# Softmax denominators in four strips of 32 columns, in an attention and feed-forward kernel

## The chip, the cores and the metric

The kernel runs on one core of one Trainium2 chip. The metric is the device time of one launch, in microseconds. A core has five engines that run side by side and wait for one another by semaphores: TensorE (matrix products, PE in the profile), VectorE (DVE), ScalarE (ACT), Pool (GpSimd, POOL) and SyncE (SP, which here issues the transfers).

## The reference

Attention with routing, and a bilinear feed-forward layer on its result. A query sees only the keys that have the same nearest centroid.

```python
batch, n_heads, seq, head_dim, n_clusters = 4, 8, 768, 64, 16     # fp32
# q_n, k_n, c_n: q, k and centroids, each row normalized
q_assign = np.argmax(np.einsum('bhsd,hcd->bhsc', q_n, c_n), axis=-1)
k_assign = np.argmax(np.einsum('bhsd,hcd->bhsc', k_n, c_n), axis=-1)
mask = q_assign[:, :, :, None] == k_assign[:, :, None, :]
scores = np.where(mask, scale * q @ k.T, -1e9)
attn = np.exp(scores - max)
attn = attn / (np.sum(attn, axis=-1, keepdims=True) + 1e-09)
x = (attn @ v)                     # (B,H,S,D) -> (B*S, H*D) = 3072 x 512
out = ((x @ w_a) * (x @ w_b)) @ w_out     # d_ff = 1536
```

What the change touches is the division by `np.sum(attn)`.

## The kernel before: what the change touches

The kernel works through 16 pairs of heads (4 batches, HP = 4 pairs each), each in two halves of HB = 384 queries. Keys lie on the partitions, in NJ = 6 tiles of 128; the two heads `a` of a pair lie side by side. A "group" `g` of the main loop handles two of the twelve key tiles of a pair, so a pair has six groups, and `l` is the group's place in its pair.

For each key tile the scores go through the exponential on ScalarE (`probs`), are summed over the key tiles into `acc` (VectorE, and Pool for later pairs) and are weighed with v on TensorE (line 581). The sum over the 128 keys of a tile is a matrix product with ones (line 604). It leaves the denominator of each query in all of the head's 64 partitions:

```python
def denominators(p, hf):
    ps = ps_m.tile([P, 512], FP32, name="m")
    acc = accs.pop((p, hf))
    terms = [acc]
    if p < HP:                       # first batch: the last key tile isn't in acc
        terms.append(probs[p * UPP + hf * NJ + NJ - 1])
    for n, t in enumerate(terms):
        for a in range(2):
            nc.tensor.matmul(out=ps[a * D:(a + 1) * D, 0:HB], lhsT=ones,      # line 604
                             rhs=t[:, a, :], start=(n == 0),
                             stop=(n == len(terms) - 1))
    den = acc[:, 0, :]
    n = 4 * p + 2 * hf
    nc.scalar.activation(out=den, in_=ps[:, 0:HB], func=AF.Copy,              # line 609
                         accum_out=stat[:, n:n + 1])
    den_of[p, hf] = acc
```

The inverse is then made on few elements. VectorE transposes blocks of 32 x 32, so that 32 equal rows become 32 equal columns, takes the reciprocal of one column of each block, and transposes back from a broadcast. Pool multiplies:

```python
def normalize(p, hf):
    ...
    den, once = acc[:, 0, :], acc[:, 1, :]
    x = xTs[b][:, hp, hf * HB:(hf + 1) * HB]
    inv = small.tile([P, HB // 32], FP32, name="inv")

    def across():
        nc.vector.transpose(out=once, in_=den)                                # line 624
    def invert():
        nc.vector.reciprocal(                                                 # line 627
            out=inv, in_=once.rearrange("p (j t) -> p j t", t=32)[:, :, 0])
    def back():
        nc.vector.transpose(out=den,                                          # line 631
            in_=inv[:, :, None].broadcast_to((P, HB // 32, 32)))
    def apply():
        nc.gpsimd.tensor_tensor(out=x, in0=x, in1=den, op=ALU.mult)           # line 636
        unchecked.append((4 * p + 2 * hf + 1, inv))
    return [across, invert, back, apply]
```

The similarities of queries and keys to the centroids (line 358) already stand in four strips of 32 columns:

```python
for kq in range(4):
    nc.tensor.matmul(out=ps[32 * kq:32 * kq + 32, 0:HB], lhsT=cTb[:, hp, :],  # line 358
                     rhs=qkTs[p][:, kq * HB:(kq + 1) * HB], start=True, stop=True)
```

The main loop (cut) issues small steps from the list `todo`, one after each piece of the feed-forward layer, and the rest at the group's end:

```python
for g in range(NG + 3):
    ...                              # scores, sums (line 570), weighing (line 581)
    if g < NG:
        ready[l]()                   # preparing the next pair; line 358 is here
    late = int(g > EARLY)
    if g % 3 == late and 0 < g - late:
        denominators(*divmod(g // 3 - 1, 2))
    ...
    ph = {first: (p, 0), second: (p - 1, 1)}.get(l)
    halved = ph in den_of
    if halved:
        todo.extend(normalize(*ph))
    if ffn:
        ...
        while len(ffn) > least and credit > 0:
            cost, piece = ffn.popleft()
            credit -= cost
            piece()
            if todo:
                todo.popleft()()
            round_next()
    ...
    while todo:
        todo.popleft()()
    if halved:
        ffn_ready(*ph)               # at a batch's end: its feed-forward pieces
```

At the end of a batch its feed-forward layer begins with combinations of x on VectorE (line 725), which need the normalized x. Its products are lines 664 and 764 (up) and 883 (down). For PSUM there are three buffers `m` that denominators, similarities, transposes and the feed-forward layer share. `acc` has two buffers and `inv` two.

Of the kernel before, what the change touches and what calls it, by code (L numbers as in the profile page):

```python
# [8 lines left out]
FP32 = mybir.dt.float32  # L9
# [4 lines left out]
AF = mybir.ActivationFunctionType  # L14
ALU = mybir.AluOpType
# [15 lines left out]
P = 128  # L31
# [105 lines left out]
def short_path(nc, tc, ctx, c, cn, centroids_in, casts, n_far, q, k, v,  # L137
# [3 lines left out]
    B, H, S, D = q.shape  # L141
# [3 lines left out]
    HP = H // 2  # L145
    NPAIR = B * HP
    NCH = DM // P
    NF = DF // P
    HB = S // 2

    def pool(name, bufs, space=None):
        kw = {} if space is None else {"space": space}
        return ctx.enter_context(tc.tile_pool(name=name, bufs=bufs, **kw))
# [9 lines left out]
    small = pool("small", 2)  # L163
# [11 lines left out]
    ident, identb, ones, rank = c["ident"], c["identb"], c["ones"], c["rank"]  # L175
# [10 lines left out]
    def by_blocks(p):  # L186
        return p >= HP
# [164 lines left out]
    def prep_sim(p):  # L352
# [4 lines left out]
        for kq in range(4):  # L357
            nc.tensor.matmul(out=ps[32 * kq:32 * kq + 32, 0:HB],  # L358
                             lhsT=cTb[:, hp, :],
                             rhs=qkTs[p][:, kq * HB:(kq + 1) * HB],  # L360
                             start=True, stop=True)
        if by_blocks(p):
            sims[p] = ps
            return
        t = simp.tile([P, HB], FP32, name="sim")
        nc.scalar.copy(out=t, in_=ps[:, 0:HB])
        sims[p] = t

    def prep_across(p):
        ps = ps_m.tile([P, 512], FP32, name="m")  # L370
        for t in range(3):
            nc.tensor.transpose(out=ps[:, t * P:(t + 1) * P],
                                in_=sims[p][:, t * P:(t + 1) * P],
                                identity=ident)
        return ps
# [52 lines left out]
    def prep_onehot_first(kq):  # L428
# [3 lines left out]
        for n in (3, 4, 5, 0, 1, 2):  # L432
# [3 lines left out]
                                identity=identb)  # L436
        c0 = kq * HB
        nc.scalar.activation(out=ohTs[0][:, S + c0:S + c0 + HB],
                             in_=ps[:, HB:S], func=AF.Identity, scale=FAR,
# [58 lines left out]
    def prep_steps(p):  # L498
        if p >= NPAIR:
            return [lambda: None] * 6  # L500

        def both(*fs):
            return lambda: [f() for f in fs]

        if by_blocks(p):
            steps = prep_by_blocks(p)
            ready = [lambda s=s: todo.extend(s) for s in steps]
            ready[1] = both(lambda: prep_sim(p), lambda: load_v(p), ready[1])
            return ready

        return [
            both(lambda: prep_transpose(p, 0), lambda: prep_transpose(p, 1)),
            both(lambda: prep_sim(p), lambda: load_v(p)),
            lambda: todo.extend(prep_assign(prep_across(p))),
            lambda: None,
            lambda: prep_onehot(p, 1),
            lambda: None,
        ]
# [2 lines left out]
    probs, accs, O_of, den_of, xTs = {}, {}, {}, {}, {}  # L521
    unchecked = []
    todo = deque()
    UPP = 2 * NJ
    NU = NPAIR * UPP

    def where(u):
        p, l = divmod(u, UPP)
        hf, j = divmod(l, NJ)
        return p, hf, j  # L530

    def score(us):
        tiles = [ps_s.tile([P, 2, 512], FP32, name="s") for _ in us]

        def add(Ts, start):
            for u, s in zip(us, tiles):
                p, hf, j = where(u)
                for a in range(2):
                    r = slice(a * D, (a + 1) * D)
                    nc.tensor.matmul(  # L540
                        out=s[:, a, 0:HB],
                        lhsT=Ts[p][r, S + j * P:S + (j + 1) * P],
                        rhs=Ts[p][r, hf * HB:(hf + 1) * HB],
                        start=start, stop=not start)

        def exp():
            for u, s in zip(us, tiles):
                pt = ptp.tile([P, 2, HB], FP32, name="pt")
                nc.scalar.activation(out=pt, in_=s[:, :, 0:HB], func=AF.Exp,  # L549
                                     scale=SCALE)  # L550
                probs[u] = pt

        if us[0] == 0:
            add(qkTs, True)
            return lambda: [add(ohTs, False), exp()]
        add(ohTs, True)
        add(qkTs, False)
        exp()
# [35 lines left out]
    def denominators(p, hf):  # L594


        ps = ps_m.tile([P, 512], FP32, name="m")
        acc = accs.pop((p, hf))
        terms = [acc]
        if p < HP:  # L600
            terms.append(probs[p * UPP + hf * NJ + NJ - 1])
        for n, t in enumerate(terms):
            for a in range(2):
                nc.tensor.matmul(out=ps[a * D:(a + 1) * D, 0:HB], lhsT=ones,  # L604
                                 rhs=t[:, a, :], start=(n == 0),
                                 stop=(n == len(terms) - 1))
        den = acc[:, 0, :]
        n = 4 * p + 2 * hf
        nc.scalar.activation(out=den, in_=ps[:, 0:HB], func=AF.Copy,
                             accum_out=stat[:, n:n + 1])  # L610
        den_of[p, hf] = acc

    def normalize(p, hf):

        b, hp = divmod(p, HP)
        acc = den_of.pop((p, hf))
        den, once = acc[:, 0, :], acc[:, 1, :]
        x = xTs[b][:, hp, hf * HB:(hf + 1) * HB]
        inv = small.tile([P, HB // 32], FP32, name="inv")

        def across():
            nc.vector.transpose(out=once, in_=den)

        def invert():
            nc.vector.reciprocal(
                out=inv, in_=once.rearrange("p (j t) -> p j t", t=32)[:, :, 0])

        def back():  # L630
            nc.vector.transpose(  # L631
                out=den,
                in_=inv[:, :, None].broadcast_to((P, HB // 32, 32)))

        def apply():
            nc.gpsimd.tensor_tensor(out=x, in0=x, in1=den, op=ALU.mult)  # L636
            unchecked.append((4 * p + 2 * hf + 1, inv))

        return [across, invert, back, apply]

    def check_inverses():
        while unchecked:
            n, inv = unchecked.pop()
            nc.scalar.activation(out=inv, in_=inv, func=AF.Copy,
                                 accum_out=stat[:, n:n + 1])


    ffn = deque()
# [334 lines left out]

    GPP = UPP // 2
    NG = NPAIR * GPP
# [33 lines left out]
    across = prep_across(0)  # L1019
# [10 lines left out]
    for g in range(NG + 3):  # L1030
        p, l = divmod(g, GPP)
        if l == 0:
            ready = prep_steps(p + 1)
        now = (2 * g, 2 * g + 1)
        before = (2 * g - 2, 2 * g - 1)
        if 0 < g < NG:
            score(now)
        check_inverses()
        if 0 < g <= NG:
            for u in before:  # L1040
                add_up(u)
        flush_w()
        if 0 < g <= NG:
            weigh(before)
        if g < NG:
            ready[l]()
        late = int(g > EARLY)
        if g % 3 == late and 0 < g - late:
            denominators(*divmod(g // 3 - 1, 2))
        parts = due.get(g, [])  # L1050

        def round_next():
            if parts:
                i = parts.pop(0)
                round_w(i)
                load_w(i + 2)

        round_next()
        if g <= EARLY:
            first, second = 4, 1  # L1060
        else:
            first, second = 5, 3 if g < NG else 2
        ph = {first: (p, 0), second: (p - 1, 1)}.get(l)
        halved = ph in den_of
        if halved:
            todo.extend(normalize(*ph))
        if ffn:
            credit += PER_GROUP[(g > 2 * BG + 3) + (g > 3 * BG + 3)]
            least = FREE_ROOM if halved and ph[1] and (ph[0] + 1) % HP == 0 else 0
# [7 lines that stand above are left out]
        else:  # L1077
            credit = 0
# [4 lines that stand above are left out]
            ffn_ready(*ph)  # L1083
        if l == 0 and p + 1 < NPAIR:
            if not by_blocks(p + 1):
                prep_transpose(p + 1, 2)
            load(p + 2)
        if l == 4 and p + 1 < NPAIR and not by_blocks(p + 1):
            prep_onehot(p + 1, 0)

    def some_ffn(n):
        for _ in range(n):
# [15 lines left out]
    ps = ps_m.tile([P, 512], FP32, name="m")  # L1108
    nc.tensor.matmul(out=ps[0:1, 0:1], lhsT=far_off, rhs=ones[:, 0:1],
                     start=True, stop=True)  # L1110
# [227 lines left out]
```

## Time and profile before

| | |
|---|---|
| time, median of 3 runs | 1072.6 us (1072.07 to 1073.93) |
| span of the profiled run | 1072.3 us |
| instructions | 13072 |
| mean granted TensorE clock | 0.995 of full speed |
| the denominators' matmuls (line 604) | 160 records, from 30.2 to 875.5 us |
| ScalarE's eviction of them (line 609) | 32, 489 ns each |
| VectorE's transpose (line 624) | 32, 568 ns each |
| reciprocal (line 627) | 32, 221 ns each |
| transpose back (line 631) | 32, 574 ns each |
| Pool's product (line 636) | 32, 1033 ns each |

How to read the profile: in a group such as `m<-acc,ones 128*64 128x384` the output stands left of the arrow and the inputs right of it; 128\*64 are the rows and columns of the array that the matrix product uses, 128x384 the partitions and columns that stream through it. A product of fp32 leaves two records in the trace. Records of matmuls overlap, so the time of a group is read from the start of the next one, not from its length. "Idle before" with an arrow names what the engine waited for. The chain of work is followed back from the last instruction: at each step to what released it.

### The profile page before, as it was taken

What the parts mean: (1) busy time and instruction counts of PE and PEld (TensorE: products, weight loads), DVE (VectorE), ACT (ScalarE), POOL (GpSimd) and SP (SyncE); (2) the same over time, 40 slices, a digit from 0 to 9 for tenths busy, and PEclk for the clock granted to TensorE, in tenths of its full rate; (3) what the DMA queues carried; (4) which work ended last, traced back from release to release, by engine and by line L of the source; (5) the groups of instructions that cost most, each with busy time, mean ns of one, the idle gap of its engine ahead of it and who ended that gap; (6) DMA issues with size and microseconds to landing.
All of it is one profiled execution on the core that took longest, in us unless ns stands there. A gap on an engine that the chain in (4) does not pass through costs nothing.

```text
span 1072.3 us, 13072 instructions
## 1 busy us (share of the span) xinstructions
PE 1054.1 (98%) x4756; PEld 607.3 (57%) x4756; DVE 708.9 (66%) x1402; ACT 260.0 (24%) x501; POOL 354.6 (33%) x329
## 2 busy tenths in 40 slices
PE   8999999999999999999999999999999999999997
PEld 5444445554557664454545766455455687555686
DVE  5778877787857446666667746667665745676762
ACT  4665333233322221212122121221212200000000
POOL 1111345454533232434445422344344410221200
PEclk9999999999999999999999999999999999999999
DMA  5334243525130210202020030300000000000000
GB/s 169 91 63 108 83 103 101 125 67 139 61 47 20 43 37 14 45 4 45 3 46 1 24 65 14 55 1 19 1 4 1 6 30 25 0 1 1 0 31 32
DMA packets 120504, 46.18 MB, mean 43 GB/s; under 512 B 106608, under 2 KB 115824, under 8 KB 120432
## 3 DMA queue, kind: packets, MB, share of 16 engines
q1 hardware_dynamic: 120016, 44.85, 17.8%
q8 instruction: 39, 0.64, 0.2%
q10 hardware_dynamic: 416, 0.43, 0.1%
q14 instruction: 33, 0.27, 0.1%
HBM read 37.78 MB, written 6.29 MB: 41 GB/s over the span
## 4 chain that ended last, share of the span: by engine, by line
PE 93%; DVE 6%; issue 1%; DMA 0%; POOL 0%; ACT 0%; DVEq 0%; POOLq 0%
PE m L764 30%; PE m L883 19%; PE s L540 14%; PE O L581 12%; PE m L664 12%; PE m L604 3%; PE m L358 1%; DVE raw L725 1%; DVE raw L747 1%; PE m L342 1%; DVE acc L570 0%; DVE xT L725 0%; DVE size L725 0%; DVE ha L774 0%; DVE sim L407 0%
## 5 line engine op out<-in xcount | busy, mean ns | idle before, releaser
L549 ACT ACTIVATE pt<-s 128x768 f32<-128x768 f32 x192 | 145.3, 809 | 314.6 <-PE s L540 260.6
L570 POOL TENSOR_TENSOR acc<-acc,pt 128x384 f32<-128x384 f32 x144 | 152.2, 1071 | 59.7 <-ACT pt L549 43.5
L779 POOL TENSOR_TENSOR h<-h,ha 128x384 f32<-128x384 f32 x72 | 72.7, 1018 | 235.6 <-DVE ha L774 234.1
L581 PE MATMUL O<-pt,v 128*64 128x384 f32 x768 | 145.1, 499 | 0.0
L540 PE MATMUL s<-qkT 64*128 64x384 f32 x768 | 141.1, 487 | 0.0
L774 DVE TENSOR_TENSOR ha<-ha,m 128x384 f32<-128x384 f32 x126 | 66.8, 546 | 74.1 <-PE m L764 73.3
L774 DVE TENSOR_TENSOR h<-h,m 128x384 f32<-128x384 f32 x126 | 67.3, 548 | 71.8 <-PE m L764 71.0
L570 DVE TENSOR_TENSOR acc<-acc,pt 128x384 f32<-128x384 f32 x96 | 73.9, 796 | 37.2 <-POOL acc L570 35.1
L581 PEld LDWEIGHTS O<-pt,v 128*64 128x64 f32 x768 | 46.6, 136 | 86.9 <-issue 85.3
L540 PEld LDWEIGHTS s<-qkT 64*128 64x128 f32 x768 | 71.3, 189 | 32.0 <-issue 1.1
L883 PE MATMUL m<-wo_sb,h 128*128 128x256 f32 x384 | 87.5, 382 | 0.0
L636 POOL TENSOR_TENSOR xT<-xT,acc 128x384 f32<-128x384 f32 x32 | 33.0, 1033 | 153.5 <-DVE acc L631 119.5
L883 PEld LDWEIGHTS m<-wo_sb,h 128*128 128x128 f32 x384 | 72.1, 190 | 16.0 <-issue 4.2
L764 PE MATMUL m<-raw 128*128 128x384 f32 x192 | 70.2, 488 | 0.9 <-DVE ha L774 0.9
L664 PE MATMUL m<-xT,wa_sb 128*128 128x384 f32 x192 | 67.1, 492 | 0.0
L664 PE MATMUL m<-xT,wb_sb 128*128 128x384 f32 x192 | 66.8, 491 | 0.0
L883 PE MATMUL m<-xT,h 128*128 128x256 f32 x288 | 65.4, 382 | 0.1
L883 PEld LDWEIGHTS m<-xT,h 128*128 128x128 f32 x288 | 54.1, 190 | 11.7 <-issue 1.7
L764 PE MATMUL m<-xT,wa_sb 128*128 128x384 f32 x144 | 53.0, 491 | 0.0
L764 PE MATMUL m<-xT,size 128*128 128x384 f32 x144 | 52.8, 490 | 0.0
L764 PE MATMUL m<-xT,wb_sb 128*128 128x384 f32 x144 | 52.8, 490 | 0.0
L664 PEld LDWEIGHTS m<-xT,wa_sb 128*128 128x128 f32 x192 | 35.5, 190 | 29.4 <-issue 3.6
(164 smaller groups left out, 1451.6 us busy)
## 6 DMA issues: line engine op xcount, KB each, us to landing
raw<-in_moe_w_a_dram SPq DMA_DIRECT2D x12, 512.0 KB, 4.3
raw<-in_moe_w_b_dram SPq DMA_DIRECT2D x12, 512.0 KB, 3.5
raw<-in_moe_w_out_dram SPq DMA_DIRECT2D x12, 512.0 KB, 3.2
qk<-in_q_dram SPq DMA_DIRECT2D x48, 96.0 KB, 2.9
qk<-in_k_dram SPq DMA_DIRECT2D x48, 96.0 KB, 3.5
v<-in_v_dram SPq DMA_DIRECT2D x24, 192.0 KB, 3.8
out_dram<-rest SPq DMA_DIRECT2D x24, 128.0 KB, 1.7
v<-in_v_dram SPq DMA_DIRECT2D x4, 384.0 KB, 4.5
```

Of the source, the lines that this page charges most:

```text
L342: nc.tensor.transpose(out=ps[:, n * P:(n + 1) * P], in_=qks[p][:, w, j].rearrange("p a d -> p (a d)"), identity=ident)
L540: nc.tensor.matmul(out=s[:, a, 0:HB], lhsT=Ts[p][r, S + j * P:S + (j + 1) * P], rhs=Ts[p][r, hf * HB:(hf + 1) * HB], start=start, stop=not ...
L549: nc.scalar.activation(out=pt, in_=s[:, :, 0:HB], func=AF.Exp, scale=SCALE)
L570: eng.tensor_tensor(out=acc[:, a, :], in0=probs[u - 1][:, a, :] if j == 1 else acc[:, a, :], in1=probs[u][:, a, :], op=ALU.add)
L581: nc.tensor.matmul(out=O_of[0][a * D:(a + 1) * D, 0:HB], lhsT=vs[p][:, a, j, :], rhs=probs[u][:, a, :], start=(j == 0), stop=(j == NJ - 1))
L604: nc.tensor.matmul(out=ps[a * D:(a + 1) * D, 0:HB], lhsT=ones, rhs=t[:, a, :], start=(n == 0), stop=(n == len(terms) - 1))
L636: nc.gpsimd.tensor_tensor(out=x, in0=x, in1=den, op=ALU.mult)
L664: nc.tensor.matmul(out=ps[:, 0:HB], lhsT=w_sb[:, ch, f * P:(f + 1) * P], rhs=xTs[b][:, ch, t0:t0 + HB], start=(ch == 0), stop=(ch == NCH - 1))
L764: nc.tensor.matmul(out=ps[:, 0:HB], lhsT=A[l][c], rhs=rhs[c], start=(c == 0), stop=(c == 1))
L774: nc.vector.tensor_tensor(out=out, in0=in0, in1=ps, op=op)
L779: nc.gpsimd.tensor_tensor(out=to, in0=to, in1=box[name], op=ALU.mult)
L883: nc.tensor.matmul(out=ps[:, 0:HN], lhsT=A[l][f // 3][:, f % 3, :], rhs=B[r][f // 2][:, f % 2, :], start=(f == 0), stop=(f == N2 - 1))
```

## The change

A denominator needs to be in only 32 partitions of a head for the block transpose to work on it, and not in 64. So the 64 partitions of a head are split into two strips of 32, and each strip gets the denominators of half the queries: strip `(a, i)` holds head `a`, queries `i * 192` to `(i + 1) * 192`. Four matmuls of 32 columns and 192 streamed elements take the place of two of 64 columns and 384. The change is meant to let TensorE stream half as many columns, and ScalarE's eviction and VectorE's first transpose handle half as many too.

After the reciprocal each strip has the inverses of its half only, but x needs all of them in both strips of a head. The reciprocal writes its six values twice, and Pool copies over the half that the strip lacks from the other strip: four copies of 32 x 6. The transpose back and the product stay as they were. As the transpose back now depends on Pool, it is put off: in the first pairs to the next group (`held`), later by an empty step in the list.

```diff
+    QB = HB // 2
...
         for n, t in enumerate(terms):
             for a in range(2):
-                nc.tensor.matmul(out=ps[a * D:(a + 1) * D, 0:HB], lhsT=ones,
-                                 rhs=t[:, a, :], start=(n == 0),
-                                 stop=(n == len(terms) - 1))
-        den = acc[:, 0, :]
+                for i in range(2):
+                    nc.tensor.matmul(out=ps[(2 * a + i) * 32:(2 * a + i + 1) * 32, 0:QB],
+                                     lhsT=ones[:, 0:32],
+                                     rhs=t[:, a, i * QB:(i + 1) * QB],
+                                     start=(n == 0), stop=(n == len(terms) - 1))
+        den = acc[:, 0, 0:QB]
...
-        nc.scalar.activation(out=den, in_=ps[:, 0:HB], func=AF.Copy,
+        nc.scalar.activation(out=den, in_=ps[:, 0:QB], func=AF.Copy,
...
-        den, once = acc[:, 0, :], acc[:, 1, :]
+        den, once, inverse = acc[:, 0, 0:QB], acc[:, 1, 0:QB], acc[:, 0, :]
...
         def invert():
+            column = once.rearrange("p (j t) -> p j t", t=32)[:, :, 0]
             nc.vector.reciprocal(
-                out=inv, in_=once.rearrange("p (j t) -> p j t", t=32)[:, :, 0])
+                out=inv.rearrange("p (i j) -> p i j", i=2),
+                in_=column[:, None, :].broadcast_to((P, 2, n)))
+
+            for r in range(0, P, 32):
+                i = r // 32 % 2
+                other = r + 32 - 64 * i
+                nc.gpsimd.tensor_copy(out=inv[r:r + 32, (1 - i) * n:(2 - i) * n],
+                                      in_=inv[other:other + 32, (1 - i) * n:(2 - i) * n])
 
         def back():
             nc.vector.transpose(
-                out=den,
-                in_=inv[:, :, None].broadcast_to((P, HB // 32, 32)))
+                out=inverse,
+                in_=inv[:, :, None].broadcast_to((P, 2 * n, 32)))
...
-        return [across, invert, back, apply]
+        return [across, invert], [back, apply]
...
+        todo.extend(held)
+        held.clear()
         late = int(g > EARLY)
...
-            todo.extend(normalize(*ph))
+
+            one, other = normalize(*ph)
+            todo.extend(one)
+            if ffn or ph[0] >= HP - 1:
+                todo.extend([lambda: None] + other)
+            else:
+                held.extend(other)
```

(In the diff `n` in `normalize` is `QB // 32`, 6.)

More of the change, by code (lines that the diff above doesn't have):

```diff
@@ L523, in short_path @@
     todo = deque()
+    held = []
     UPP = 2 * NJ
@@ L616, in normalize @@
         acc = den_of.pop((p, hf))
-        den, once = acc[:, 0, :], acc[:, 1, :]
+        den, once, inverse = acc[:, 0, 0:QB], acc[:, 1, 0:QB], acc[:, 0, :]
         x = xTs[b][:, hp, hf * HB:(hf + 1) * HB]
-        inv = small.tile([P, HB // 32], FP32, name="inv")
+        n = QB // 32
+        inv = small.tile([P, 2 * n], FP32, name="inv")
         def across():
@@ L626, in invert @@
         def invert():
+            column = once.rearrange("p (j t) -> p j t", t=32)[:, :, 0]
             nc.vector.reciprocal(
-                out=inv, in_=once.rearrange("p (j t) -> p j t", t=32)[:, :, 0])
+                out=inv.rearrange("p (i j) -> p i j", i=2),
[5 more added lines that the diff above has]
+                                      in_=inv[other:other + 32, (1 - i) * n:(2 - i) * n])
         def back():
             nc.vector.transpose(
-                out=den,
-                in_=inv[:, :, None].broadcast_to((P, HB // 32, 32)))
+                out=inverse,
+                in_=inv[:, :, None].broadcast_to((P, 2 * n, 32)))
         def apply():
-            nc.gpsimd.tensor_tensor(out=x, in0=x, in1=den, op=ALU.mult)
+            nc.gpsimd.tensor_tensor(out=x, in0=x, in1=inverse, op=ALU.mult)
             unchecked.append((4 * p + 2 * hf + 1, inv))
-        return [across, invert, back, apply]
+        return [across, invert], [back, apply]
     def check_inverses():
```

## The prediction

> **What bounds the kernel now.** I read the views in this order: busy shares, the chain of work that ended last, the groups by line and form, then the timeline of TensorE around single denominators, and last the timeline of all engines at the two places where TensorE stands still. First the busy shares of the page:
>
> ```profile
> PE 1054.1 (98%) x4756; PEld 607.3 (57%) x4756; DVE 708.9 (66%) x1402; ACT 260.0 (24%) x501; POOL 354.6 (33%) x329
> ...
> PE 93%; DVE 6%; issue 1%; DMA 0%; POOL 0%; ACT 0%; DVEq 0%; POOLq 0%
> PE m L764 30%; PE m L883 19%; PE s L540 14%; PE O L581 12%; PE m L664 12%; PE m L604 3%; PE m L358 1%; DVE raw L725 1%; DVE raw L747 1%; PE m L342 1%; DVE acc L570 0%; DVE xT L725 0%; DVE size L725 0%; DVE ha L774 0%; DVE sim L407 0%
> ```
>
> TensorE is busy for 1054 of 1072.3 us and carries 93% of the chain. A microsecond of TensorE time is therefore a microsecond of the kernel, nearly everywhere. Line 604, the denominators, is on the chain with 3%, some 30 us: that is the ceiling of what this change can bring. VectorE has 34% slack, Pool 67%. A wait there costs something only where the chain runs through VectorE.
>
> Next, TensorE's timeline (start, length, engine, line, group) around a denominator that follows the weighing (L581), and around one that follows the similarities (L358), and one of the early ones with two terms:
>
> ```profile
> 527.18 1.51 PE L581 MATMUL O<-pt,v 128*64 128x384 f32 x8
> 528.52 0.82 PE L604 MATMUL m<-acc,ones 128*64 128x384 f32 x4
> 529.27 1.56 PE L764 MATMUL m<-xT,wa_sb 128*128 128x384 f32 x4
> ```
> ```profile
> 557.26 1.51 PE L581 MATMUL O<-pt,v 128*64 128x384 f32 x8
> 558.70 0.85 PE L358 MATMUL m<-qkT,cTb 128*32 128x384 f32 x8
> 559.48 0.87 PE L604 MATMUL m<-acc,ones 128*64 128x384 f32 x4
> 560.28 1.56 PE L764 MATMUL m<-raw 128*128 128x384 f32 x4
> ```
> ```profile
> 128.46 0.81 PE L604 MATMUL m<-acc,ones 128*64 128x384 f32 x4
> 129.10 0.81 PE L604 MATMUL m<-pt,ones 128*64 128x384 f32 x4
> 129.85 1.56 PE L664 MATMUL m<-xT,wb_sb 128*128 128x384 f32 x4
> ```
>
> Lengths overlap, so differences of starts are what counts. Each fp32 matmul leaves two records, two passes. A denominator with one term takes 529.27 - 528.52 = 0.75 us after L581, and 0.80 us after L358; two terms take 129.85 - 128.46 = 1.39 us. The first term's step (129.10 - 128.46 = 0.64 us) is two passes of 384 columns, 0.32 us each, for both 64-column halves together: the two halves already run side by side. L358 is the pattern that the change brings: four strips of 32 columns, 384 columns each, in 559.48 - 558.70 = 0.78 us, no more than two strips of 64 need. A change of strip width has a price: L581 lasts 1.34 us ahead of L604 (same width, 528.52 - 527.18) but 1.44 us ahead of L358.
>
> Last, the boundary between two batches, where TensorE stands still (VectorE and then Pool and TensorE, same columns, idle time and releaser in brackets):
>
> ```profile
> 396.24 0.57 DVE L624 STREAM_TRANSPOSE acc<-acc 128x384 f32<-128x384 f32 x1
> 396.84 0.23 DVE L627 RECIPROCAL inv<-acc 128x12 f32<-128x12 f32 x1
> 397.11 0.58 DVE L631 STREAM_TRANSPOSE acc<-inv 128x384 f32<-128x384 f32 x1
> 398.87 0.56 DVE L570 TENSOR_TENSOR acc<-pt 128x384 f32<-128x384 f32 x1 [1.19 <-POOL xT L636]
> ```
> ```profile
> 397.83 1.01 POOL L636 TENSOR_TENSOR xT<-xT,acc 128x384 f32<-128x384 f32 x1 [6.90 <-DVE acc L631]
> ```
> ```profile
> 408.54 1.62 PE L764 MATMUL m<-raw,comb 128*128 128x384 f32 x4 [2.20 <-DVE comb L747]
> 665.75 2.81 PE L764 MATMUL m<-raw,comb 128*128 128x384 f32 x4 [2.20 <-DVE comb L747]
> ```
>
> Here the whole normalization is on the chain: transpose, reciprocal, transpose back, Pool's product, then VectorE's first sum, which needs the buffer that Pool frees, then the combining of x, and TensorE waits 2.20 us at its end. It happens twice (batches 1 and 2; at batch 3 there are no sums left to wait).
>
> **What the Trainium skill says.** "TensorE: Matmul & The Clock Gate", Part 3 (packing small matmuls): matmuls on different column groups run concurrently, and three strips of 32 columns gave 2.38 times the throughput. The trace agrees, by L358 above. "TensorEngine Tiling (Array Packing)", Key Properties: changing the tiling mode, not just the tile, drains the engine. The trace agrees in size: 1.44 against 1.34 us. "GPSIMD Engine Reference", 2.1 (instruction dispatch): each Pool instruction passes a broadcast and a software dispatcher, so small ones pay for dispatch. The page of before has only a few small Pool instructions, a 128x1 memset at 99 ns and the 128x16 iota at 142 ns; nothing yet shows a copy between partitions. "TensorE: Matmul & The Clock Gate", Part 1: after an idle window of 3.4 us the clock falls to one half. The trace shows that too: the granted clock is 0.50 in the stretches 409.9 to 413.3 and 665.9 to 669.3 us, right behind the two stops.
>
> **The change part by part.** TensorE first. Four strips of 192 columns halve the passes to 0.16 us. From L358, 0.78 - 2 x 0.16 = 0.46 us for one term with its switches; a second term adds 2 x 0.16 = 0.32. By the program's order the 32 denominators fall into these groups:
> - 13 with one term after L581: 1.34 + 0.75 becomes 1.44 + 0.46, so 0.19 us less each, 2.5 us. The new switch from 64 to 32 columns eats 0.10 of it.
> - 10 with one term after L358: 0.78 + 0.80 becomes about 0.68 + 0.45, because the switch between the two goes. 0.45 us less each, 4.5 us.
> - 1 after L883: 0.80 to 0.46, 0.3 us.
> - 6 with two terms after L581: 1.34 + 1.39 becomes 1.44 + 0.78, 0.51 us less each, 3.0 us. Four of them wait for the sums on VectorE first; the gain comes after the wait.
> - 2 with two terms after the transposes L342: 1.44 to 0.78, 0.66 us less each, 1.3 us.
>
> Sum: 11.6 us off TensorE.
>
> ScalarE evicts 192 columns in place of 384: from 489 ns (384, L609) to about 326, by the slope of its plain copies (588 ns for 512, 479 for 384). It is no bound, no gain. VectorE's transpose of L624 goes from 568 ns to an estimated 370: 128x768 takes 963 and 128x384 568, 1.03 ns a column. That is 6.3 us of VectorE work over 32, worth something only where VectorE is the chain. The reciprocal still writes 12 elements a partition (221 ns), and the transpose back stays whole (574 ns).
>
> Pool gets 128 copies of 32x6. I estimate 100 to 140 ns each from the memset and the iota, so 0.4 to 0.56 us a normalization and 13 to 18 us in all, on an engine that idles 717 us. What matters is the round trip in front of the transpose back. For the first three pairs it is put off to the next group, with 4 to 6 us of VectorE work between; later a slot is left empty between. In the built order the transpose back still follows the reciprocal directly on VectorE in 13 of 32 places; there VectorE waits. At the boundary: Pool answers 0.14 us after its releaser (397.83 against 397.69), four copies take 0.48, VectorE answers in 0.03. The transpose back starts about 0.65 us after the reciprocal's end and not 0.04: +0.61, less 0.20 for the shorter transpose. So +0.4 us on the chain at each of two boundaries, +0.8 us.
>
> In the first 110 us three of the four waits of L604 for its sums have a normalization in VectorE's stretch before them; 0.2 us less work there gives about -0.5 us in all. For the other direct waits, above all where Pool is still in a weight's sum of 1.3 us (L290 ends up to 0.75 us after the reciprocal around 146, 185 and 244 us), VectorE loses up to 1.4 us each time. TensorE has three PSUM buffers ahead of it, so I charge only +0.5 us for all.
>
> Net: -11.6 + 0.8 - 0.5 + 0.5 = -10.8 us, 1072.6 to about 1062.
>
> **The rivals.** One: four strips don't run side by side at 192 columns, because eight loads and eight passes are bound by issue. Then a denominator takes what it takes now, the extra switch costs 0.1 us at 19 places after L581, and the time is about 1074. Against it: at L358 four strips start within 0.02 us of each other. Two: VectorE's wait for Pool becomes a wait of TensorE, because Pool works in order and takes 1 to 1.3 us for each sum or product ahead of the copies. If all 13 direct places passed 1 us on, the gain is gone: 1075. For it: at the boundaries it is certain. Against: away from the boundaries VectorE waits for Pool already, 1.11 us for L636 at 228 us and 2.09 us for a sum of Pool's at 188 us on its timeline, and TensorE has no stop near either. Three: the two stops grow past another clock window, and 3.4 us more at half clock cost 1.7 us each: 1064 to 1066. The reverse, a window missed, gives 1059 to 1060.
>
> **Range and chances.** The 11.6 us could be 9 to 13, since the 192-column pass is scaled and not seen; the waits 0 to +4; the clock windows -3 to +3. I predict 1062 us, range 1058.5 to 1067. Two per cent is 21 us, nearly twice the whole TensorE gain, so faster by that has 1%; slower by 21 us needs a stall at every normalization, 2%.
>
> **What would show it.** On TensorE's timeline, L608 (the new line of the denominators) should take 0.46 us and L581 ahead of it 1.44. The group of 32x6 copies on Pool should show 100 to 140 ns each; at 250 ns or more each boundary gains another half microsecond of stop. TensorE's waits at the two boundaries should read about 2.6 us in place of 2.20. If TensorE's busy time falls by 11 us but the span doesn't, rival two is right, and new waits of TensorE for VectorE, or of VectorE for line 641, will carry the difference. If the denominators stay at 0.75 us, rival one is.

## The result

The changed kernel takes 1075.4 us (median of 6, 1074.0 to 1075.8) against 1072.0 us (median of 6, 1070.5 to 1073.9) for the kernel before. The ratio is 1.0028, 95% interval 1.0015 to 1.0041. It was predicted at 1062 us, with a range of 1058.5 to 1067. It is 0.3% slower where 1% faster was forecast.

### The profile page after: what moved, and what is told of

It is laid out like the page before. It is cut to its first block, busy times and chain, and to the rows that moved or that the text cites. A ratio compares the mean times of both kernels' runs of the same rounds, so it can differ in the third digit from the quotient of the medians.

```text
span 1072.1 us, 13572 instructions
## 1 busy us (share of the span) xinstructions
PE 1045.3 (97%) x4916; PEld 605.1 (56%) x4916; DVE 704.4 (66%) x1402; ACT 254.9 (24%) x501; POOL 386.3 (36%) x457
## 4 chain that ended last, share of the span: by engine, by line
PE 81%; DVE 12%; POOL 3%; issue 3%; DMA 0%; ACT 0%; DVEq 0%; POOLq 0%
PE m L778 30%; PE m L897 18%; PE s L542 12%; PE O L583 10%; PE m L678 6%; DVE acc L572 1%; PE m L608 1%; PE m L359 1%; DVE raw L739 1%; POOL acc L572 1%; DVE wa_sb L298 1%; DVE raw L761 1%; DVE rest L286 1%; POOL wa_sb L291 1%; PE m L343 0%
## 5 line engine op out<-in xcount | busy, mean ns | idle before, releaser
L572 DVE TENSOR_TENSOR acc<-acc,pt 128x384 f32<-128x384 f32 x96 | 77.7, 836 | 42.2 <-POOL acc L572 40.0
L641 POOL COPY inv<-inv 32x6 f32<-32x6 f32 x128 | 30.5, 238 | 140.0 <-DVE inv L634 135.0
L778 PEld LDWEIGHTS m<-raw 128*128 128x128 f32 x192 | 36.1, 190 | 27.4 <-DVE ha L788 2.1
```

The source lines that it names most:

```text
L572: eng.tensor_tensor(out=acc[:, a, :], in0=probs[u - 1][:, a, :] if j == 1 else acc[:, a, :], in1=probs[u][:, a, :], op=ALU.add)
L641: nc.gpsimd.tensor_copy(out=inv[r:r + 32, (1 - i) * n:(2 - i) * n], in_=inv[other:other + 32, (1 - i) * n:(2 - i) * n])
L778: nc.tensor.matmul(out=ps[:, 0:HB], lhsT=A[l][c], rhs=rhs[c], start=(c == 0), stop=(c == 1))
```

## The profile after

First the busy shares of the page of the changed kernel, the shares of the chain, and the new group on Pool:

```profile
PE 1045.3 (97%) x4916; PEld 605.1 (56%) x4916; DVE 704.4 (66%) x1402; ACT 254.9 (24%) x501; POOL 386.3 (36%) x457
...
PE 81%; DVE 12%; POOL 3%; issue 3%; DMA 0%; ACT 0%; DVEq 0%; POOLq 0%
...
L641 POOL COPY inv<-inv 32x6 f32<-32x6 f32 x128 | 30.5, 238 | 140.0 <-DVE inv L634 135.0
```

TensorE is busy for 8.8 us less, although it spent 3.4 us more at half clock (shown below), so the gain was made. The chain no longer runs on TensorE alone: VectorE and Pool carry 15% in place of 6%. A copy of 32x6 takes 238 ns.

TensorE's timeline around the same three kinds of denominator (line 604 is now 608, 581 is 583, 358 is 359):

```profile
528.55 1.51 PE L583 MATMUL O<-pt,v 128*64 128x384 f32 x8
529.99 0.53 PE L608 MATMUL m<-acc,ones 128*32 128x192 f32 x8
530.46 1.56 PE L778 MATMUL m<-xT,wa_sb 128*128 128x384 f32 x4
```
```profile
559.88 0.85 PE L359 MATMUL m<-qkT,cTb 128*32 128x384 f32 x8
560.55 0.51 PE L608 MATMUL m<-acc,ones 128*32 128x192 f32 x8
560.99 1.24 PE L778 MATMUL m<-raw 128*128 128x384 f32 x3
```
```profile
94.20 0.53 PE L608 MATMUL m<-acc,ones 128*32 128x192 f32 x8
94.55 0.51 PE L608 MATMUL m<-pt,ones 128*32 128x192 f32 x8
94.99 0.50 PE L542 MATMUL s<-ohT 64*128 64x384 bf16 x4
```

Starts again: 0.47 us for one term after the weighing, 0.44 after the similarities (and those take 0.67, without the switch), 0.79 for two terms. The predicted 0.46, 0.45 and 0.78 are all there, and the weighing ahead takes the expected 1.44 us (528.55 to 529.99).

Where it went is in TensorE's waits (who waited for whom, total us, times, longest), first in the kernel before, then in the changed one:

```profile
PE m L764 <- DVE comb L747: 4.8, 3, 2.2
PE m L604 <- DVE acc L570: 2.9, 5, 1.7
```
```profile
PE m L778 <- DVE comb L761: 6.5, 3, 3.0
PE m L608 <- DVE acc L572: 4.7, 7, 0.8
PE m L359 <- DVE qkT L461: 4.0, 2, 2.1
```

The third line of the changed kernel is new: twice TensorE waits some 2 us, at 193 and at 254 us, for VectorE's transposes of q and k (the same answer for the kernel before has no such line). The first is the two boundary stops and one short wait. VectorE's timeline shows what held it up. First the kernel before, then the changed one, around the same half (reciprocal, transpose back, first sum of the next key tiles):

```profile
185.31 0.22 DVE L627 RECIPROCAL inv<-acc 128x12 f32<-128x12 f32 x1
185.57 0.58 DVE L631 STREAM_TRANSPOSE acc<-inv 128x384 f32<-128x384 f32 x1
188.24 1.34 DVE L570 TENSOR_TENSOR acc<-acc,pt 128x384 f32<-128x384 f32 x1 [2.09 <-POOL acc L570]
```
```profile
184.14 0.22 DVE L634 RECIPROCAL inv<-acc 128x12 f32<-128x12 f32 x1
186.06 0.58 DVE L645 STREAM_TRANSPOSE acc<-inv 128x384 f32<-128x384 f32 x1 [1.70 <-POOL inv L641]
188.78 1.33 DVE L572 TENSOR_TENSOR acc<-acc,pt 128x384 f32<-128x384 f32 x1 [2.14 <-POOL acc L572]
```

From the reciprocal to the sum are 2.93 us before and 4.64 us after. The wait of 1.70 us for the copies isn't absorbed by the wait for Pool's sum behind it, because Pool does its product and its sum only after the transpose back. Both waits lie in one chain that goes to and fro between VectorE and Pool. VectorE came to this half 1.17 us ahead of the kernel before, and leaves it 0.54 us behind.

Seven instructions after that sum VectorE transposes q and k. Here are these transposes and the similarities on TensorE that need them, before and after:

```profile
193.61 1.83 DVE L460 STREAM_TRANSPOSE qkT<-qk 128x768 f32<-128x768 f32 x2
196.07 0.85 PE L358 MATMUL m<-qkT,cTb 128*32 128x384 f32 x8
```
```profile
194.17 1.83 DVE L461 STREAM_TRANSPOSE qkT<-qk 128x768 f32<-128x768 f32 x2
195.19 1.38 PE L359 MATMUL m<-qkT,cTb 128*32 128x384 f32 x6 [1.91 <-DVE qkT L461]
```

TensorE comes here 2.86 us earlier than before (the weighing ahead starts at 191.77 us and not at 194.63), VectorE 0.56 us later, and so TensorE waits.

At the boundary (VectorE, then TensorE):

```profile
397.16 0.23 DVE L634 RECIPROCAL inv<-acc 128x12 f32<-128x12 f32 x1
398.34 0.58 DVE L645 STREAM_TRANSPOSE acc<-inv 128x384 f32<-128x384 f32 x1 [0.95 <-POOL inv L641]
400.03 0.56 DVE L572 TENSOR_TENSOR acc<-pt 128x384 f32<-128x384 f32 x1 [1.12 <-POOL xT L650]
```
```profile
409.71 2.93 PE L778 MATMUL m<-raw,comb 128*128 128x384 f32 x4 [3.04 <-DVE comb L761]
...
667.29 1.83 PE L778 MATMUL m<-raw,comb 128*128 128x384 f32 x4 [3.04 <-DVE comb L761]
```

Each stop grew from 2.20 to 3.04 us, and the clock stood at one half for 10.2 us behind them (three windows of 3.4 us) in place of 6.8. The windows of the changed kernel (stretch and its length, busy time of PE, PEld, DVE, ACT and POOL, granted clock, DMA):

```profile
409.04:412.45 3.41, 2.74 (x4) 1.18 (x4) 1.62 (x9) 0.00 (x0) 0.00 (x0) 0.50 0.09 23
412.45:415.86 3.41, 3.41 (x13) 1.46 (x12) 1.02 (x2) 0.81 (x1) 0.00 (x0) 0.50 0.23 72
668.45:671.86 3.41, 3.41 (x14) 1.47 (x12) 1.02 (x2) 0.60 (x1) 0.00 (x0) 0.50 0.09 24
```

How the time was won and lost along the run is seen from the starts of the 192 exponentials, as differences to the kernel before (us, minus is earlier; worked out from the traces; a shift of up to 1.2 us at the first is the prologue's):

```
exponential   before   changed   e1      e4      e9
     0         15.4     -0.3     1.2     0.3     0.7
    48        126.6     -3.3    -1.8    -2.7    -2.7
    64        204.3     -0.5    -3.0    -3.8    -3.4
    80        282.4     +1.8    -3.6    -4.5    -4.1
   104        397.1     +0.5    -4.9    -5.8    -5.4
   112        444.0     +2.0    -5.7    -7.2    -7.7
   191        856.9     -0.1    -9.3    -9.5   -13.5
```

The changed kernel is 3.3 us ahead at 127 us, loses 5.1 us by 282 us, while the weights are rounded on VectorE and Pool, loses 1.5 us at the first boundary, and gains slowly elsewhere. In the columns e1 and e9 part of the difference is clock: the profiled execution of e1 is the slowest of its four (1064.7 us; the median is 1061.0), with two windows at half clock like the kernel before, and that of e9 has none.

## The experiments

All ratios are to the kernel before on the same chip, with their 95% interval; its median there was 1073.3 to 1073.5 us.

**e1: no copies.** Strips, deferral and order stay; the four copies of each half go, so the inverses of a strip's other half are left out.

```diff
-            for r in range(0, P, 32):
+            for r in ():                      # other_half: four Pool copies
                 ...
                 nc.gpsimd.tensor_copy(out=inv[r:r + 32, ...], in_=inv[other:other + 32, ...])
```

> The changed kernel without Pool's 128 copies of 32x6; order, strips and deferral stay. It leaves out bringing the inverses of a strip's other half, so half of x is divided by other queries' denominators. Theory A (the loss is the round trip VectorE, Pool, VectorE): TensorE's gain appears, about 1063 to 1066 us, and TensorE's waits for the transposes of q and k near 193 and 254 us (2.0 and 2.1 us in the changed kernel) shrink to under 1 us each. Rival B (VectorE and Pool bound the stage of weight rounding whoever moves the inverses, so TensorE's gain there is void): 1068 to 1071 us, both waits still over 1 us. Rival C (the deferral costs, by Pool's product falling on the sums): about 1072 us.

Measured: 1061.0 us, ratio 0.9885 (0.9870 to 0.9900), 2 us below theory A's range. TensorE's waits of this run, and the busy shares:

```profile
PE m L778 <- DVE comb L761: 4.7, 3, 2.2
PE m L608 <- DVE acc L572: 4.6, 7, 0.8
...
PE 1042.6 (98%) x4916; PEld 605.3 (57%) x4916; DVE 703.3 (66%) x1402; ACT 254.9 (24%) x501; POOL 354.8 (33%) x329
```

The line for the transposes of q and k is gone altogether, and the boundary stop is at 2.2 us again. Rivals B and C fall as the main cause: with the strips and the deferral in place, VectorE keeps up. A part of rival C stays, as TensorE waits 4.6 us for the sums, like the changed kernel, and 2.9 us in the kernel before. Without the copies the kernel is 1.1% faster than the kernel before, and taking them out gains 1.4% on the changed one. Not all of this is waits: three of the four executions ran at a granted clock of 1.000, where the median is 0.997 in the kernel before and 0.9935 in the changed one (e4 says what that is worth).

**e2: the round trip alone.** The kernel before, with the copies and the deferral put in and the denominators left in two strips.

```diff
             nc.vector.reciprocal(out=inv, in_=once...)
+            for r in range(0, P, 32):
+                ...
+                nc.gpsimd.tensor_copy(out=inv[r:r + 32, (1 - i) * n:(2 - i) * n],
+                                      in_=inv[other:other + 32, (1 - i) * n:(2 - i) * n])
-        return [across, invert, back, apply]
+        return [across, invert], [back, apply]      # put off as in the changed kernel
```

> The kernel before with only the round trip: four Pool copies of 32x6 between the strips of a head (which hold equal values there) and the deferral, denominators still in two strips of 64 columns. Theory A: the round trip costs what the changed kernel lost, 12 to 15 us, so 1080 to 1087 us if its cost doesn't depend on TensorE being faster; at least 1077. Rival B: most of the loss was only TensorE's gain that found no use, so the round trip alone costs little: the two boundaries with 0.8 us each and up to 3 us of half clock, 1074 to 1077 us.

Measured: 1084.0 us, ratio 1.0100 (1.0085 to 1.0115), inside theory A's range: the round trip costs 10.7 us here. Its waits of TensorE and of VectorE hold the same lines as the changed kernel's:

```profile
PE m L358 <- DVE qkT L460: 3.4, 2, 1.8
```
```profile
DVE acc L638 <- POOL inv L634: 15.6, 13, 1.7
```

So the loss doesn't need a faster TensorE. It is there with the old strips, at the same two places. Not all of it is VectorE's wait for the copies. By the exponential at 86 us this run is 2.5 us behind the kernel before (the prologue's shift taken off), and VectorE waits for a copy for the first time at 119 us; whether the deferral or something else costs that isn't separated. From 127 to 282 us it loses another 5.9 us.

**e3: no copies at the two boundaries** (those inverses left out).

```diff
-            for r in range(0, P, 32):
+            for r in (range(0, P, 32) if (p, hf) not in ((7, 1), (11, 1)) else ()):
```

> The changed kernel without the copies at the two batch boundaries alone (second half of the last pair of batches 1 and 2); it leaves out those inverses. Each boundary's stop of TensorE should fall from 3.04 us to below the 2.20 us of before, by the 0.95 us that VectorE waits there, and the half clock behind the stops from 10.2 us in all to 6.8 or less. Theory A and B alike: 2 to 4 us less than the changed kernel, 1071.5 to 1073.5 us. If the stops stay at 3 us the boundary's chain isn't what I read.

Measured: 1071.1 us, ratio 0.9983 (0.9973 to 0.9994), 0.45% below the changed kernel's ratio, some 4.8 us. Both stops are back at 2.2 us, and not below it, where I had expected them: the 0.84 us that each lost is the wait that the copies added, 1.7 us for the two. The rest of the 4.8 us is clock, by the estimate under e4. The profiled execution, which has no window at half clock before its end, is one of the shorter of 13 (1069.1 us, of 1068.0 to 1074.0) and doesn't stand for all of them.

**e4: no copies from the fourth pair to the eighth** (but with them at 397 us; those inverses left out).

```diff
-            for r in range(0, P, 32):
+            for r in (range(0, P, 32) if not (3 <= p <= 7) or (p, hf) == (7, 1) else ()):
```

> The changed kernel without the copies from the fourth pair to the eighth (batch 1's stage with the rounding of the weights, about 100 to 375 us), but with them at the boundary at 397 us; it leaves out those inverses. Theory A: 4 to 6 us less than the changed kernel, 1069.5 to 1071.5 us, and TensorE's waits near 193 and 254 us nearly gone. Rival B: under 2 us less, 1073.5 us or more, and the waits stay.

Measured: 1065.9 us, ratio 0.9936 (0.9923 to 0.9950), 0.92% below the changed kernel's, some 9.9 us. The waits near 193 and 254 us are gone, and one near 125 us too (0.7 us in the changed kernel). It is more than theory A's 4 to 6 us.

Some of it is clock. As an estimate, the time of an execution times (1 - its granted clock) is what half clock took from it. In the median this is 3.2 us for the kernel before (0.997), 7.0 for the changed kernel (0.9935), 4.3 for e3 and for e4 (0.996) and nothing for e1 (1.000). The clock is given to a thousandth, so each of these is good to about half a microsecond. Of the 15.3 us between the changed kernel and e1 some 7 are then half clock, and some 8 are waits. Of e3's 4.8 us some 3 are half clock; of e4's 9.9 us also some 3, and some 7 are waits. The traces agree for e4. By 282 us, before either run has a window at half clock, it is 6.3 us ahead of the changed kernel, and by 857 us 9.4; its two windows fewer (one in place of three) are worth 3.4 us.

That the copies bring the windows by lengthening the stops isn't shown: e4's boundary stops are as long as the changed kernel's (3.03 us). e3 and e4 together give 14.7 us of the 15.3, so if their gains add, the first three pairs and all after the eighth but the boundaries cost next to nothing.

**e5: the round trip a group earlier.** The first transpose, the reciprocal and the copies are issued one group ahead of the transpose back, for every half.

```diff
+        early = {first - 1: (p, 0), second - 1: (p - 1, 1)}.get(l)
+        if early in den_of:
+            one, half_done[early] = normalize(*early)
+            todo.extend(one)
-        halved = ph in den_of
+        halved = ph in half_done
         if halved:
-            one, other = normalize(*ph)
-            ...
+            todo.extend(half_done.pop(ph))
```

> The changed kernel with the first transpose, the reciprocal and Pool's copies issued one group earlier than the transpose back and the product, for every half; nothing is left out. Four to thirteen VectorE instructions then lie between the reciprocal and the transpose back almost everywhere. If the loss is that VectorE waits for the round trip, the strips' whole gain appears with the copies kept: 1059 to 1064 us, no wait of VectorE for the copies over 0.5 us, and at the two boundaries a stop of TensorE below 2.2 us, as transpose and reciprocal have left that chain too. Rival (Pool's 30 us of copies themselves hold up Pool's other work): 1068 us or more.

Measured: 1067.6 us, ratio 0.9943 (0.9931 to 0.9955): faster than both kernels, but outside the range, some 7 us behind e1. VectorE no longer waits for the copies, and the boundary stops shrank to 0.4 us, both as expected. Yet VectorE waits more for Pool's sums, and TensorE has new waits of 3.0 us near 255 us, for the transposes of q and k, and of 2.4 us near 343 us. Waits of VectorE and of Pool in this run:

```profile
DVE acc L572 <- POOL acc L572: 58.6, 27, 2.8
```
```profile
POOL inv L641 <- DVE inv L634: 201.2, 31, 18.6
```

In Pool's order the copies now stand ahead of sums and weights, and Pool stood at them for 201 us in all until VectorE came to the reciprocal. Much of that costs nothing: e9 below stands at its copies for 122 us and is no slower for it. But some of it falls on sums that could have started. One such place on Pool:

```profile
232.89 1.28 POOL L291 TENSOR_TENSOR wo_sb<-wo_sb,rest 128x512 f32<-128x512 f32 x1 [2.88 <-DVE rest L286]
234.42 0.86 POOL L641 COPY inv<-inv 32x6 f32<-32x6 f32 x4 [0.25 <-DVE inv L634]
235.36 3.22 POOL L572 TENSOR_TENSOR acc<-acc,pt 128x384 f32<-128x384 f32 x3
```

The sums start 1.19 us after the end of the weight's sum (line 291). In e6, which has no copies, they follow it at once.

**e6: the same without the copies** (the other half's inverses left out; the loop over the four copies is empty as in e1).

> The same as the kernel with the round trip a group earlier, but without the copies (leaves out the inverses of the other half). Measures what the copies still cost once nothing waits for them: if the round trip is hidden, at most 2 us less than with them; if Pool's time itself matters, 4 us or more less.

Measured: 1060.3 us, ratio 0.9877 (0.9862 to 0.9891), 7.3 us below e5. VectorE's wait for the sums:

```profile
DVE acc L572 <- POOL acc L572: 25.9, 15, 2.8
```

Less than half of e5's. So the copies cost even when VectorE doesn't wait for them. Whether by their length or by their place e9 tells.

**e7: the old strips, earlier.** The kernel before with only the move of e5; no copies, no new strips.

> The kernel before (two strips of 64 columns, no copies) with the first transpose and the reciprocal issued one group earlier. Separates the move from the strips: the move alone shortens the chain at the two boundaries by some 0.8 us each and may save a clock window, so 1068 to 1072 us. If it gains as much as the strips with the move, the strips are worth nothing.

Measured: 1075.0 us, ratio 1.0017 (1.0009 to 1.0025). A miss: the boundary stops did shrink (the gap between TensorE's starts there from 2.69 to 2.34 us), but in the first 110 us, where VectorE waits for ScalarE's eviction once the transpose comes so early, TensorE's waits for the sums grew (its start-to-start gaps at 56 and 83 us from 0.81 to 1.75 and 1.79 us). The move alone gains nothing. e9 below makes the same move, so what it gains over this run comes from the strips.

**e8: small reciprocals on VectorE.** The changed kernel with VectorE reading the other strip itself; nothing is left out.

```diff
-                nc.gpsimd.tensor_copy(out=inv[r:r + 32, ...], in_=inv[other:other + 32, ...])
+                nc.vector.reciprocal(out=inv[r:r + 32, ...], in_=column[other:other + 32, :])
```

> The changed kernel, but the other half's inverses made by four more reciprocals of 32x6 on VectorE, which read the other strip, in place of Pool's copies; nothing is left out, order stays. No round trip between engines, but an estimated 0.8 us more of VectorE for each half (4 at about 0.2 us, from the 221 ns of the 128x12). Where VectorE is the chain, that is about half of the 1.3 to 1.7 us of the round trip: 1064 to 1069 us. If it is not faster than the changed kernel, the length of VectorE's chain counts and not who works on it.

Measured: 1071.0 us, ratio 0.9975 (0.9966 to 0.9985), 2 us above the expected range, though 0.5% below the changed kernel's ratio. Each takes 182 ns, 0.73 us for a half. Without any round trip the same two places still wait, only less (start-to-start gaps of 0.60 and 1.17 us near 196 and 254 us, against 2.39 and 2.54 in the changed kernel). At the two boundaries TensorE stops for 2.99 and 2.98 us, nearly as long as with the copies. What counts is by how much VectorE's chain gets longer, whoever does the work.

**e9: the copies behind the sums.** As e5, but Pool's copies are issued after the sums of the next group, when the reciprocal is long done.

```diff
+        def other_half():                          # the four Pool copies
             for r in range(0, P, 32): ...
-        return [across, invert], [back, apply]
+        return [across, invert], other_half, [back, apply]
...
                 add_up(u)
+        while copies:                              # of the halves begun a group ago
+            copies.pop()()
         flush_w()
```

> As the kernel with the round trip a group earlier, but Pool's four copies stand in its order behind the sums of the next group, when the reciprocal is long done; nothing is left out. If the 7 us between the run with the copies earlier (1067.6) and the one without (1060.3) come from Pool waiting at the copies with its sums held up behind them (201 us of Pool's waits there), this is 1060.5 to 1064 us and Pool waits under 40 us for the reciprocal. If they come from the copies' own 0.95 us on Pool or from the transpose back waiting for Pool's longer queue, it stays at 1066 to 1070 us.

Measured: 1060.9 us, ratio 0.9892 (0.9876 to 0.9909): the best use of Pool, 1.1% faster than the kernel before, with nothing left out. Waits of VectorE and of Pool:

```profile
DVE acc L572 <- POOL acc L572: 26.0, 15, 2.8
```
```profile
POOL inv L642 <- DVE inv L634: 121.9, 24, 16.0
```

VectorE's wait for the sums is at e6's value. Pool still waits 122 us at the copies, and not under 40 as I had expected; but nothing that VectorE needs soon stands behind them any more. The copies themselves even got longer (326 ns each). So it was their place in Pool's order, not their time: e6, with no copies at all, is only 0.6 us faster, and the intervals overlap.

**e10: the copies on ScalarE**, otherwise e5.

```diff
-                nc.gpsimd.tensor_copy(out=inv[...], in_=inv[...])
+                nc.scalar.copy(out=inv[...], in_=inv[...])
```

> As the kernel with the round trip a group earlier, but the four copies run on ScalarE and not on Pool; nothing is left out. Pool's sums are then held up by nothing; ScalarE may wait for the reciprocal with the next exponentials behind it. If only Pool's order matters, 1061 to 1065 us; if exponentials held up stop TensorE, over 1070 us.

Measured: 1060.5 us, ratio 0.9885 (0.9868 to 0.9901), 194 ns a copy. With the copies out of Pool's order, e5's loss is gone without any other change. ScalarE, 27% busy, stands at the copies for 128 us, but TensorE waits for an exponential only once, for 0.2 us. e9 and e10 can't be told apart.

## Why the prediction was wrong

- **TensorE's 11.6 us: right.** Each of the lengths came out within 0.02 us, and TensorE is busy for 1042.6 us in e1 against 1054.1 before, 11.5 us less, with two windows at half clock in both profiles. ScalarE's eviction (327 ns) and VectorE's first transpose (368 ns) were as estimated too. That e1's time, 1061.0 us, lies so near 1062 is partly luck, since most of its executions ran at full clock. The strips run side by side at 192 columns, and the switch of width costs 0.10 us; the first rival falls.
- **The copies, 100 to 140 ns: too low.** They take 238 ns. A half's four take 0.85 us in place of 0.48.
- **The boundaries, +0.4 us each: the term was half of what it is.** The stop grew by 0.84 us each. Of this 0.4 us is the longer copies. The third rival came true as well: by the estimate under e4 the changed kernel loses 3.8 us more at half clock than the kernel before. That the longer stops are the reason isn't shown.
- **"I charge only +0.5 us for all": the step that failed.** It assumed that a wait of VectorE reaches TensorE only through the three PSUM buffers, and that these absorb it. It doesn't come through PSUM. In the stage of weight rounding VectorE and Pool hand work to each other with hardly any slack, and the transposes of q and k, which TensorE needs at a fixed place, stand behind all of it in VectorE's order. In the kernel before, the second of them ended at 195.44 us on VectorE's timeline, and TensorE took it at 196.07: 0.6 us of slack (near 254 us, the other place, 254.50 and 254.57), on an engine that the page shows idle for a third of the time. The waits for the copies of the fourth to eighth pair cost 6.3 us by 282 us (e4, before any window at half clock), not 0.5.
- **The count of direct waits, 13, was right**, and so was the rival that named them; it was given too little weight. The argument against it, that VectorE already waits for Pool there without a stop of TensorE, was the sign to the contrary: two engines that wait for each other at every step have no slack between them. That this rival's figure, 1075, is the measured one is luck: it let all 13 waits pass on 1 us, while two places passed on some 2 us each and the clock windows came on top.
- **The waits in the first 110 us, -0.5 us:** TensorE's waits for the sums didn't fall but rose by 1.8 us in all, from 2.9 to 4.7 (the deferred product of Pool now lies beside the sums, see below).

Together, as an estimate: 5.8 us more than charged for the stage of weight rounding, 3.8 for half clock, 2.3 for the sums and 0.9 for the boundaries make 12.8 of the 14.2 us between the forecast (10.8 faster) and the result (3.4 slower).

What stays open is why the changed kernel has more windows at half clock. With boundary stops as long as its own, e2 and e4 lose an estimated 3.2 and 4.3 us to them, and the changed kernel 7.0. The windows also differ from one execution to the next in the same kernel.

## What to carry to other kernels

An engine that is idle a third of the time can be on the path of a whole stage. Before a round trip is put into its order, look for the latest instruction behind it that the bounding engine needs, and for its slack in microseconds. The small copies on Pool cost by where they stood, more than by what they took: behind the work that others wait for, all 128 cost less than 1 us; ahead of such work they cost 7 us. Leaving a cost out (e1) and putting it alone into the old kernel (e2) tell a lost gain from one that was never made. And before a difference of a few microseconds is put down to waits, take off what half clock took from each run.

## What the runs showed of the hardware

- A copy of 32 x 6 elements between partitions takes 238 ns on Pool, 194 on ScalarE; a reciprocal of that size 182 on VectorE. A reciprocal of 128 x 12, twice the elements in each partition and four times the partitions, takes 221.
- VectorE's sums take longer while Pool works on a product: the pair of sums at 55 us took 1.02 us before, with Pool idle, and 1.79 us after, with Pool's deferred product beside it.
- A stop of TensorE of 2.2 us is followed by a stretch of 3.4 us at half clock in some executions (two in the profile of before) and by none in others (e3, with stops as long). A stop of 3.04 us brought 6.8 us at half clock once, and in e5 such a stretch starts at 107 us, behind waits of TensorE of at most 1.44 us. From 30 us on, TensorE never stands still for more than 3.05 us in any of these profiles, so half clock came here without an idle window of 3.4 us, which the prediction names. By estimate each stretch costs some 1.7 us, half its length.
